# When the spread of a block's maximum is read back from its PSUM bank, in a fused window attention and gated feed-forward kernel

## The chip, the core and the metric

The kernel runs on one core of a Trainium2 chip. TensorE (PE in the profile) multiplies matrices into PSUM, VectorE (DVE) and ScalarE (ACT) work on SBUF and PSUM, GpSimd (POOL) works on SBUF, and SyncE (SP) issues the DMAs. Each engine takes its instructions in the order in which they stand in the program and waits for others by semaphores. The metric is the device time of one execution in microseconds (us).

## The reference

A softmax over 7 window weights for each token and head mixes 7 neighbouring rows of `x`; the result goes through a feed-forward layer with a sigmoid gate. There are 16384 tokens of width 192 and a hidden width of 2048.

```python
def _attn_ref(x, weight_gen):                 # x (4, 4096, 192), weight_gen (4, 4096, 8, 7)
    w = np.exp(weight_gen - np.max(weight_gen, axis=-1, keepdims=True))
    w = w / (np.sum(w, axis=-1, keepdims=True) + 1e-09)
    ...
    out = np.einsum('bshk,bskhg->bshg', w, x_unf)

def _moe_ref(x, w_in, w_out):                 # x (16384, 192)
    h = x @ w_in                              # (16384, 2048)
    g = h * (1.0 / (1.0 + np.exp(-1.702 * h)))
    return (g @ w_out).astype(np.float32)
```

## The kernel before

**Tiling.** The 16384 tokens are 32 blocks of 512. The hidden width is 16 pieces of 128. A unit is one block with one such piece, so there are 512 units, numbered in order. A unit's hidden values are one PSUM bank (128x512 fp32). Every fp32 operand is held as two fp16 parts, so the products are made of several fp16 matmuls.

**A unit's way.** `whole` (lines 391 to 394) is four 512-column matmuls into the unit's bank. `halves` (lines 403 and 404) adds, for two units at a time, two 64-row matmuls, which run side by side in the two halves of the array; a group has three such pairs. `gate` takes the tanh on ScalarE (line 409) and multiplies on VectorE into the bank (line 410). `split` makes the two fp16 parts, the first on ScalarE (line 415) and the second on VectorE (line 416), and with that the bank is free. `second` (lines 426 to 428) is the second layer: 192-column matmuls into the banks named `o`.

**Groups.** Units go in groups of six after a first group of two, with one hidden bank for each place of a group: unit number modulo 6 picks the bank `h0` to `h5`, and the first unit of a group has `h2`. PE takes in each group: `whole` of the first three units with stretches of `second` for the group before in between, the three pairs of `halves`, and then for each further unit a stretch of `second` and its `whole`. `gate` and `split` follow unit by unit.

**A block's scale.** Before its units begin, a block's attention output (GpSimd, lines 149 and 164) gets a power of two as a scale. `scales` takes the largest absolute value per partition on VectorE (line 234), turns it and reduces it again (lines 202 and 207), and a one-column matmul with ones (line 210) spreads it over all partitions, into a whole PSUM bank: `h2`, or an `o` bank for block 1. VectorE reads that bank back (line 216), which frees it, and makes the scale's bits (lines 220 to 222). Then ScalarE and VectorE scale and split the block (`split_x`, lines 275 and 278), and SyncE turns it by DMA into `xt` and copies part of it into `xd` (`turn`, lines 284 and 288).

**What sets the order.** The order is written by hand: `plan(slots, generator)` lists a time for each step of a generator, counted in units, and `until(t)` in the main loop issues all steps that are due before `t`. `first(n)` is the first unit of the group in which unit `n` lies. For a block whose first group starts at `n`, the matmul of line 210 has the time `n - 7.4` and the read of line 216 the time `n - 7.39`: that is the second group before, place 4 (the fifth unit), at 0.6. In the loop the fifth unit's gate is issued, then steps due before 0.5, then the split of the fourth unit, then steps due before the next whole number:

```python
                gate(u)
                until(n + 0.5 + i)
                if last:
                    split(last)
                last = u
                until(min(n + 1 + i, z - 0.4))
```

In the first three groups VectorE and ScalarE also prepare the second layer's weights (`parts_out`, lines 358, 360 and 378).

Of the kernel before, what the change touches and what calls it, by code (L numbers as in the profile page):

```python
# [22 lines left out]
def conv_attention_then_ffn(  # L23
# [10 lines left out]
    B, S, D = x.shape  # L34
    H, K = wg.shape[2], wg.shape[3]
# [9 lines left out]
    NF = DFF // P  # L45
# [178 lines left out]
    def scales(blk):  # L224

        s = scale[blk] = spool.tile([P, 8], F32, tag="s", name="s")
        t = tops[blk % 2]
        if blk == 0:
            for c, n in ((0, P), (1, C1)):
                nc.vector.tensor_reduce(  # L230
                    t[0:n, c : c + 1], turned[c][0:n, :], axis=AX.X, op=ALU.max, apply_absolute_value=True
                )
        else:
            nc.vector.tensor_reduce(
                t[:, 0:1], xa[blk].rearrange("p j d -> p (j d)"), axis=AX.X, op=ALU.max, apply_absolute_value=True
            )
        e = s[:, 0:1].bitcast(I32)
        yield from top_of(t, e, False, ("h3", "o")[blk] if blk < 2 else "h2")
        yield
        power(e, s[:, 2:3], s[:, 3:4], 263)  # L240
# [165 lines left out]
    def gate(u):  # L406

        t = gpool.tile([P, N], F32, tag="th", name="th", bufs=2)
        nc.scalar.activation(t, hp[u], AF.Tanh, scale=scale[u[0]][:, 4:5])  # L409
        nc.vector.scalar_tensor_tensor(hp[u], t, 1.0, hp[u], ALU.add, ALU.mult)  # L410
# [41 lines left out]
    def plan(slots, gen):  # L452
        for n in slots:
            todo.setdefault(math.floor(n), []).append((n, len(todo), gen))

    def once(fn, *args):
        fn(*args)
        yield
# [12 lines left out]
    def hold(t):  # L471

        nc.gpsimd.tensor_copy(held, t)

    with tc.manual_schedule():
        load_w(0)
        load_x(0, 0, J)
        load_tail(0)
        load_in(0)
        load_in(1)  # L480
        load_x(0, J, XB * J)
        load_in(2)
        load_tail(1)
        load_in(3)
        for c in range(4):
            load_out(c)
        load_w(1)
        load_x(1, 0, XB * J)
        constants()


        w_first = ps_h.tile([P, N], F32, tag="h0", name="w")[:, 0 : J * H * K].rearrange("p (n k) -> p n k", k=K)
        plan((-36.1, -35.7, -35.1, -34.6, -33.6), softmax(0, V, w_first))
        plan((-35.3, -34.7, -33.9, -33.2, -32.0), softmax(1, G_))
        plan((-36.2,), once(warm, 7, ident, P))
        plan((-32.1, -30.4, -27.7, -25.0), attend_first(w_first))
        plan((-24.9, -24, -23, -22, -21, -0.04, -0.03), attend(1))
        plan((-20.5, -18.3, -17.1, -17.1), scales(0))
        plan((-15.7, -13.6), split_first())
        raw = {"t": raw_t, "i": raw_i, "o": [raw_o[:, c * QC : (c + 1) * QC] for c in range(NO)]}  # L500
        for k, c, at, *slots in (
            ("t", 0, 0, -28.6, -23.2, -21.6),
            ("i", 0, 1, -27.4, -21.8, -19.7),
            ("i", 1, 2, -26.2, -18.4, -16.9),
            ("i", 2, 3, -24.6, -16.3, -14.5),
            ("t", 1, 4, -22.3, -14.9, -13.2),
            ("i", 3, 5, -20.4, -12.1, -10.1),
            ("o", 0, 6, -18.5, -10.7, -8.9),
            ("o", 1, 7, -13.9, -9.4, -7.5),
            ("o", 2, 8, -12.0, -7.2, -5.7),  # L510
            ("o", 3, 9, -10.8, -4.8, -0.6),
            ("o", 4, 10, -8.2, -0.05, 1.4),
            ("o", 5, 11, -6.3, 1.45, 1.9),
        ):
            plan(slots, narrow((k, c), raw[k][c], at))
        plan((-8.0, -7.1, -5.8), bound_in())
        plan((-5.0,), scales_gate(0))
        plan((-4.5, -3.5), parts_tail(0))
        plan((-3.8, -2.8), parts_in(0))
        plan((-0.05,), once(hold, w0l[:, DFF - 8 :]))  # L520
        plan((-2.75,), once(warm, 5, w0h, QC))
        plan((-3.2, -2.1), parts_in(1))
        plan((-2.5, -1.4), parts_tail(1))
        plan((-1.9, -0.7), parts_in(2))
        plan((-1.2, -0.06), parts_in(3))
        plan((1.95, 4.6, 4.65), bound_out())
        for c, slots in enumerate(((4.7, 5.2), (5.3, 5.8), (6.2, 6.7), (7.55, 7.9), (7.95, 8.1), (8.2, 8.6))):
            plan(slots, parts_out(c))
        plan((4.66,), scales_out(0))
        plan((7.7, 9.4, 9.45, 9.46), scales(1))  # L530
        plan((9.47,), scales_gate(1))
        plan((9.48,), scales_out(1))
        plan((9.49, 10.6), split_x(1))
        plan((10.65, 12), turn(1))

        for blk in range(2, NB):
            n = first(blk * NF)
            plan([n - 12.2, n - 7.4, n - 7.39, n - 7.38], scales(blk))
            plan([n - 6.28], scales_gate(blk))
            plan([n - 6.26], scales_out(blk))  # L540
            plan([n - 6.3, n - 6.2], split_x(blk))
            plan([n - 6.15, n - 5], turn(blk))
            if blk == 2:
                plan((-0.04, 0.5, 4.9, 6.4, 7.2, 7.25), softmax(blk, G_))
                plan((8.61,), once(lambda: hold(wos[:, NF * D - 8 :])))
                plan([8.62 + k for k in range(K)], attend(blk))
            elif blk == 3:
                plan((5.9, 7.26, 8.7, 10.7, 13.7, 17.6), softmax(blk, G_))
                plan([18 + 2 * k for k in range(K)], attend(blk))
            else:  # L550
                plan([n - 48.2, n - 48.1, n - 42.1, n - 36.15, n - 30.2, n - 30.1], softmax(blk, G_))
                plan([n - 30 + 2.2 * k for k in range(K)], attend(blk))
            if blk % XB == 0 and blk > XB:
                plan([blk * NF - 56.5], load_pair(blk // XB))

        def seconds(six):


            for z in zip(six[::2], six[1::2]):
                blk, f = z[0]  # L560
                for i in range(2):
                    if f in (0, NF - 2):
                        for j in (2 * i, 2 * i + 1):
                            for u in z:
                                second(u, j)
                        if f:
                            store(blk, i, each=blk == NB - 1)
                    else:
                        for j in range(J):
                            second(z[i], j)  # L570
                    yield

        sixes = [units[:few]] + [units[n : n + Q] for n in range(few, len(units), Q)]
        for k, us in enumerate([None] + sixes, -1):
            n, z = (min(todo), 0) if k < 0 else (units.index(us[0]), units.index(us[-1]) + 1)
            steps = sorted((t for i in range(n, z) for t in todo.get(i, ())), key=lambda t: t[:2])

            def until(end):
                while steps and steps[0][0] < end:
                    next(steps.pop(0)[2], None)  # L580

            if k < 0:
                until(z)
                continue
            due = seconds(sixes[k - 1] if k > 2 else sixes[0] + sixes[1] if k == 2 else ())
            early, late = us[:3], us[3:]
            if len(us) < Q:
                early, late = us, []
            for i, u in enumerate(early):
                bank(u)  # L590
                whole(u, True, False)
                if i == 1 or i == 0 and k > 2:
                    next(due, None)
                    until(n + 0.5 + 0.5 * i)
            for u in late:
                bank(u)
            for u, v in zip(us[::2], us[1::2]):
                halves(u, v, u in early, v in early)
            last = None
            for i, u in enumerate(us):  # L600
                if i > 1:
                    next(due, None)
                if u in late:
                    whole(u, False, True)
                gate(u)
                until(n + 0.5 + i)
                if last:
# [4 lines that stand above are left out]
            until(z)  # L612
            for _ in due:
                pass
        for _ in seconds(sixes[-1]):
            pass
# [29 lines left out]
```

## Time and profile before

| | us |
|---|---|
| median of 3 runs | 1102.25 (1102.07 to 1102.97) |
| the profiled execution, its own time | 1101.69 |
| its span, first to last instruction | 1099.7 |
| PE busy in it | 1050.0 (95%) |
| DVE busy | 886.6 (81%) |
| POOL busy | 721.2 (66%) |
| ACT busy | 703.6 (64%) |

The span is one execution as the profiler saw it; the time of that execution is 2.0 us longer than its span. Busy time is the union of the records of an engine. A PE record is longer than the distance to the next one, because matmuls are pipelined and the ends of their records are modelled: so the start of one matmul against the start of the next tells how fast PE goes, and idle time counted from the end of a record is less than what was lost.

### The profile page before, as it was taken

Reading aid. Unit: us, or ns where it says so; the run is one execution under the profiler, and the core shown is the slowest. Engines: PE = TensorE matmul, PEld = TensorE weight load, DVE = VectorE, ACT = ScalarE, POOL = GpSimd, SP = SyncE. Lnnn points to the kernel's source line nnn. Section 1 sums busy time; section 2 is a strip of 40 time slices with the busy share of each in tenths; the row PEclk is TensorE's granted clock in tenths of the full one; section 3 lists DMA queues with packets and bytes.
Section 4 is the critical chain, followed back from the end, with each engine's and each line's share of the span. In section 5 each row is a group of like instructions: output and inputs, shape, how many; then the busy total and the mean of one; then the engine's idle time right before and its main releaser. Section 6 shows DMA issues by size and latency. Waiting matters only on the chain.

```text
span 1099.7 us, 22223 instructions
## 1 busy us (share of the span) xinstructions
PE 1050.0 (95%) x8821; PEld 732.6 (67%) x8821; DVE 886.6 (81%) x1556; ACT 703.6 (64%) x1251; POOL 721.2 (66%) x484
## 2 busy tenths in 40 slices
PE   4579999999999999999999999999999999999998
PEld 3146766676667676667766667666666766676666
DVE  8887877888797888879787877887887788788765
ACT  5765666666666666666666666656666666567655
POOL 4469758686855868685587768558775856786100
PEclk9689999999999999999999999999999999999999
DMA  9300120312012121301212120131212102101010
GB/s 305 119 17 16 39 83 18 91 32 91 15 32 77 32 91 32 87 18 32 76 33 90 32 80 27 32 77 32 88 35 74 33 17 91 33 21 44 15 30 18
DMA packets 73231, 60.71 MB, mean 55 GB/s; under 512 B 60588, under 2 KB 65964, under 8 KB 71592
## 3 DMA queue, kind: packets, MB, share of 16 engines
q1 hardware_dynamic: 73128, 59.30, 18.7%
q8 instruction: 69, 1.13, 0.4%
q14 instruction: 34, 0.28, 0.1%
HBM read 31.96 MB, written 12.58 MB: 41 GB/s over the span
## 4 chain that ended last, share of the span: by engine, by line
PE 83%; DVE 8%; ACT 6%; issue 2%; DMA 0%; ACTq 0%
PE o L426 14%; PE o L427 14%; PE o L428 14%; PE h L391 9%; PE h L392 9%; PE h L394 9%; PE h L393 9%; PE h L403 5%; DVE h L410 4%; ACT th L409 3%; DVE g L416 3%; ACT osb L435 1%; DVE tap L149 0%; ACT abs L337 0%; ACT g L415 0%
## 5 line engine op out<-in xcount | busy, mean ns | idle before, releaser
L426 PE MATMUL o<-wos,g 128*128 128x192 f16 x2048 | 505.7, 247 | 3.2 <-DVE s L216 3.2
L427 PE MATMUL o<-wol,g 128*128 128x192 f16 x2048 | 504.9, 247 | 0.5 <-DVE wol L360 0.5
L428 PE MATMUL o<-woh,g 128*128 128x192 f16 x2048 | 504.8, 246 | 0.0
L410 DVE SCALAR_TENSOR_TENSOR h<-th,h 128x512 f32<-128x512 f32 x512 | 347.0, 693 | 181.7 <-ACT th L409 174.6
L409 ACT ACTIVATE th<-h,s 128x512 f32<-128x512 f32 x512 | 342.4, 686 | 231.8 <-PE h L404 135.8
L416 DVE SCALAR_TENSOR_TENSOR g<-g,h 128x512 f16<-128x512 f16 x512 | 349.2, 682 | 13.7 <-ACT g L415 2.0
L164 POOL TENSOR_TENSOR acc<-acc,prod 128x768 f32<-128x768 f32 x186 | 346.3, 1862 | 14.6
L415 ACT ACTIVATE g<-h 128x512 f16<-128x512 f32 x512 | 305.0, 596 | 44.1 <-DVE h L410 44.1
L149 POOL TENSOR_TENSOR prod<-xb,wb 128x768 f32<-128x768 f32 x186 | 288.9, 1553 | 11.1
L426 PEld LDWEIGHTS <-g 128*128 128x128 f16 x2048 | 200.4, 98 | 75.7 <-issue 35.9
L427 PEld LDWEIGHTS <-g 128*128 128x128 f16 x2048 | 200.6, 98 | 39.5 <-issue 3.2
L391 PE MATMUL h<-xt,w0l 128*128 128x512 f16 x512 | 195.1, 381 | 10.4 <-DVE s L216 10.4
L428 PEld LDWEIGHTS <-g 128*128 128x128 f16 x2048 | 200.7, 98 | 0.8 <-issue 0.7
L394 PE MATMUL h<-xt,wth 128*128 128x512 f16 x512 | 195.1, 381 | 0.0
L393 PE MATMUL h<-xt,w0h 128*128 128x512 f16 x512 | 195.1, 381 | 0.0
L392 PE MATMUL h<-xt,w0h 128*128 128x512 f16 x512 | 195.1, 381 | 0.0
L143 POOL TENSOR_TENSOR wb<-wb,wr 128x224 f32<-128x224 f32 x31 | 17.9, 576 | 229.1 <-DVE wr L140 225.6
L278 DVE SCALAR_TENSOR_TENSOR xs<-acc,s,xs 128x512 f16<-128x512 f32 (+1 forms) x62 | 102.3, 1689 | 0.0
L394 PEld LDWEIGHTS <-wth 128*128 128x128 f16 x512 | 50.3, 98 | 61.1 <-issue 1.1
L393 PEld LDWEIGHTS <-w0h 128*128 128x128 f16 x512 | 50.2, 98 | 61.1 <-issue 1.1
L403 PE MATMUL h<-xt,tl 64*128 64x512 f16 x256 | 70.6, 381 | 2.4 <-DVE g L416 2.4
L404 PE MATMUL h<-xd,tl 64*128 64x512 f16 x256 | 70.7, 381 | 2.0 <-DVE g L416 2.0
(92 smaller groups left out, 523.2 us busy)
## 6 DMA issues: line engine op xcount, KB each, us to landing
xb<-in_x_dram SPq DMA_DIRECT2D x12, 1344.0 KB, 6.4
out_dram<-osb SPq DMA_DIRECT2D x31, 384.0 KB, 2.4
wb<-in_weight_gen_dram SPq DMA_DIRECT2D x16, 224.0 KB, 3.2
ro<-in_moe_w_out_dram SPq DMA_DIRECT2D x4, 768.0 KB, 12.3
xb<-in_x_dram SPq DMA_DIRECT2D x3, 768.0 KB, 7.4
ri<-in_moe_w_in_dram SPq DMA_DIRECT2D x4, 512.0 KB, 8.6
xb<-in_x_dram SPq DMA_DIRECT2D x4, 504.0 KB, 5.2
xd<-xt SPq DMA_DIRECT2D x31, 64.0 KB, 2.1
```

The costliest lines, as they stand in the source:

```text
L164: nc.gpsimd.tensor_tensor(acc, acc, t, ALU.add)
L391: nc.tensor.matmul(ps, lhsT=w0l[:, s], rhs=x0, start=start, stop=False)
L392: nc.tensor.matmul(ps, lhsT=w0h[:, s], rhs=x2, start=False, stop=False)
L393: nc.tensor.matmul(ps, lhsT=w0h[:, s], rhs=x0, start=False, stop=False)
L394: nc.tensor.matmul(ps, lhsT=th_[:, s], rhs=x1, start=False, stop=stop)
L409: nc.scalar.activation(t, hp[u], AF.Tanh, scale=scale[u[0]][:, 4:5])
L410: nc.vector.scalar_tensor_tensor(hp[u], t, 1.0, hp[u], ALU.add, ALU.mult)
L415: nc.scalar.activation(g[:, 0], hp[u], AF.Copy, scale=2.0**-12)
L416: nc.vector.scalar_tensor_tensor(g[:, 1], g[:, 0], -(2.0**12), hp.pop(u), ALU.mult, ALU.add)
L426: nc.tensor.matmul(o, lhsT=lo, rhs=wos[:, d], start=a and j % 2 == 0, stop=False, skip_group_check=True)
L427: nc.tensor.matmul(o, lhsT=hi, rhs=wol[:, d], start=False, stop=False, skip_group_check=True)
L428: nc.tensor.matmul(o, lhsT=hi, rhs=woh[:, d], start=False, stop=z, skip_group_check=True)
```

## The change

Nothing is computed in another way. The diff gives three kinds of steps other places in the order.

- For blocks 2 to 31 the spread and its read are due at `n - 7.9` and `n - 7.89`, the three bit operations at `n - 7.3`. A new `until(n + 0.25 + i)` ahead of every gate issues steps that are due in the first quarter of a place. With both, matmul and read stand ahead of the fifth unit's gate; the bit operations stay behind the fourth unit's split.
- For block 1 (`scales(1)`) the spread and its read are due at 8.9 and 8.91 in place of 9.4 and 9.45, which is before the third `whole` of that group.
- Some weight preparation of the second group moves: the steps at 8.1 and 8.6 of the last two `parts_out` come at 8.92 and 8.96, the start of block 2's attention comes at 8.97, and the new `until` lets steps due in a first quarter (at 5.2, 6.2 and 7.2) pass one gate.

```diff
-        for c, slots in enumerate(((4.7, 5.2), (5.3, 5.8), (6.2, 6.7), (7.55, 7.9), (7.95, 8.1), (8.2, 8.6))):
+        for c, slots in enumerate(((4.7, 5.2), (5.3, 5.8), (6.2, 6.7), (7.55, 7.9), (7.95, 8.92), (8.2, 8.96))):
             plan(slots, parts_out(c))
         plan((4.66,), scales_out(0))
-        plan((7.7, 9.4, 9.45, 9.46), scales(1))
+        plan((7.7, 8.9, 8.91, 9.46), scales(1))
...
-            plan([n - 12.2, n - 7.4, n - 7.39, n - 7.38], scales(blk))
+            plan([n - 12.2, n - 7.9, n - 7.89, n - 7.3], scales(blk))
...
-                plan((8.61,), once(lambda: hold(wos[:, NF * D - 8 :])))
-                plan([8.62 + k for k in range(K)], attend(blk))
+                plan((8.97,), once(lambda: hold(wos[:, NF * D - 8 :])))
+                plan([8.98 + k for k in range(K)], attend(blk))
...
+                until(n + 0.25 + i)
                 gate(u)
                 until(n + 0.5 + i)
```

VectorE's order before, in the group in which block 2's maximum is read. The names: `h` and `th` are the hidden bank and its tanh (line 410 is a gate), `g` the fp16 parts (line 416 is a split), `top` the bank with the spread maximum and `s` the block's scale. `h_994` is the fifth unit of the group:

```order
L410 SCALAR_TENSOR_TENSOR h_993<-th_1050,h_993 128x512
L416 SCALAR_TENSOR_TENSOR g_1053<-g_1053,h_988 128x512
L410 SCALAR_TENSOR_TENSOR h_994<-th_1072,h_994 128x512
L416 SCALAR_TENSOR_TENSOR g_1078<-g_1078,h_993 128x512
L216 TENSOR_SCALAR s_939<-top_1081 128x1
L220 TENSOR_SCALAR s_939<-s_939 128x1
```

The same place on VectorE now:

```order
L410 SCALAR_TENSOR_TENSOR h_993<-th_1050,h_993 128x512
L416 SCALAR_TENSOR_TENSOR g_1053<-g_1053,h_988 128x512
L216 TENSOR_SCALAR s_939<-top_1075 128x1
L410 SCALAR_TENSOR_TENSOR h_994<-th_1078,h_994 128x512
L416 SCALAR_TENSOR_TENSOR g_1081<-g_1081,h_993 128x512
L220 TENSOR_SCALAR s_939<-s_939 128x1
```

The read has moved ahead of one gate and one split; so it is in all of blocks 2 to 31, and PE's order is the same there.

PE's order before, around block 1's spread. The names: `o` is a bank of the second layer, `top_624` the spread in an `o` bank, `xd` and `xt` the block's input:

```order
L403 MATMUL h_610<-xt_314,tl_114 128x512
L404 LDWEIGHTS tl_114
L404 MATMUL h_611<-xd_317,tl_114 128x512
L210 LDWEIGHTS ones_92
L210 MATMUL top_624<-tf_566,ones_92 128x1
L426 LDWEIGHTS g_443
L426 MATMUL o_640<-wos_99,g_443 128x192
```

The same matmul on PE now:

```order
L428 LDWEIGHTS g_446
L428 MATMUL o_582<-woh_97,g_446 128x192
L210 LDWEIGHTS ones_92
L210 MATMUL top_597<-tf_566,ones_92 128x1
L391 LDWEIGHTS w0l_95
L391 MATMUL h_607<-xt_314,w0l_95 128x512
L392 LDWEIGHTS w0h_94
L392 MATMUL h_607<-xt_314,w0h_94 128x512
```

The spread has moved ahead of the third `whole` of the group and the six matmuls of `halves` behind it; it is the one place where PE's order differs.

## Rows read from the trace of the kernel before

**Rows 1.** The page's first part: busy time of each engine, share of span, instructions.

```profile
PE 1050.0 (95%) x8821; PEld 732.6 (67%) x8821; DVE 886.6 (81%) x1556; ACT 703.6 (64%) x1251; POOL 721.2 (66%) x484
```

**Rows 2.** The waits: engine, line, waited for; total, times, longest (us).

```profile
PE h L391 <- DVE s L216: 10.4, 30, 0.3
PE o L426 <- DVE s L216: 3.2, 1, 3.2
```

**Rows 3.** Timeline around 420 us: start, length (us), engine, line; idle before, releaser.

```profile
418.66 0.17 PE L210 MATMUL top<-tf,ones 128*128 128x1 bf16 x1
...
419.64 0.70 DVE L410 SCALAR_TENSOR_TENSOR h<-th,h 128x512 f32<-128x512 f32 x1 [0.57 <-ACT th L409]
...
420.24 0.68 DVE L416 SCALAR_TENSOR_TENSOR g<-g,h 128x512 f16<-128x512 f16 x1
...
420.32 0.38 PE L394 MATMUL h<-xt,wth 128*128 128x512 f16 x1
...
420.84 0.15 DVE L216 TENSOR_SCALAR s<-top 128x1 int32<-128x1 int32 x1
...
421.05 0.38 PE L391 MATMUL h<-xt,w0l 128*128 128x512 f16 x1 [0.35 <-DVE s L216]
...
421.26 0.38 PE L392 MATMUL h<-xt,w0h 128*128 128x512 f16 x1
```

**Rows 4.** Timeline: PE at the first and the last of the 30 such places.

```profile
103.54 0.38 PE L394 MATMUL h<-xt,wth 128*128 128x512 f16 x1
...
104.26 0.38 PE L391 MATMUL h<-xt,w0l 128*128 128x512 f16 x1 [0.34 <-DVE s L216]
...
1041.39 0.38 PE L394 MATMUL h<-xt,wth 128*128 128x512 f16 x1
...
1042.11 0.38 PE L391 MATMUL h<-xt,w0l 128*128 128x512 f16 x1 [0.35 <-DVE s L216]
```

**Rows 5.** Timeline of DVE before the fifth gate of another such group, around 163 us.

```profile
163.13 0.68 DVE L416 SCALAR_TENSOR_TENSOR g<-g,h 128x512 f16<-128x512 f16 x1
163.82 0.69 DVE L410 SCALAR_TENSOR_TENSOR h<-th,h 128x512 f32<-128x512 f32 x1
```

**Rows 6.** Timeline, two deliveries that PE needs soon: a turned block, a freed bank.

```profile
699.80 0.62 SPq L288 DMA_DIRECT2D xd<-xt  x1
...
700.83 0.38 PE L391 MATMUL h<-xt,w0l 128*128 128x512 f16 x1
...
508.00 1.44 DVE L416 SCALAR_TENSOR_TENSOR g<-g,h 128x512 f16<-128x512 f16 x2
...
511.07 0.38 PE L404 MATMUL h<-xd,tl 64*128 64x512 f16 x1
```

**Rows 7.** Timeline of the start, 57 to 85 us, around block 1's spread.

```profile
57.12 0.24 PE L427 MATMUL o<-wol,g 128*128 128x192 f16 x1 [0.52 <-DVE wol L360]
...
65.45 0.16 PE L210 MATMUL top<-tf,ones 128*128 128x1 bf16 x1 [0.72 <-DVE tf L207]
...
66.66 1.24 ACT L409 ACTIVATE th<-h,s 128x512 f32<-128x512 f32 x2
...
68.77 0.32 PE L426 MATMUL o<-wos,g 128*128 128x192 f16 x1 [3.15 <-DVE s L216]
...
72.23 0.38 PE L391 MATMUL h<-xt,w0l 128*128 128x512 f16 x1
...
80.12 0.62 SPq L288 DMA_DIRECT2D xd<-xt  x1
...
84.66 0.38 PE L403 MATMUL h<-xt,tl 64*128 64x512 f16 x1
```

**Rows 8.** Stretches: window, length, busy time and count by engine, PE's granted clock, DMA.

```profile
61.60:71.90 10.30, 4.75 (x24) 3.30 (x24) 9.16 (x22) 8.72 (x16) 6.40 (x6) 0.50 0.00 0
80.00:1095.00 1015.00, 1004.65 (x8557) 704.15 (x8556) 817.84 (x1414) 647.74 (x1146) 681.41 (x443) 1.00 0.17 48
```

**Rows 9.** The page's sixth part, DMA issues: count, KB each, us to landing.

```profile
xd<-xt SPq DMA_DIRECT2D x31, 64.0 KB, 2.1
```

## The prediction

> **What bounds the kernel now.** I read the page's busy times first, then the list of waits, then the timeline at the longest PE waits, and last the stretches with the granted clock. TensorE bounds it: PE is busy for 95% of the span and no other engine for more than 81% [rows 1]. So what counts is where PE stands still. The list of waits has two entries that concern the read of a block's maximum (line 216): PE's first `whole` matmul of a group waits for it 30 times, 10.4 us in all, and one `second` matmul waits 3.2 us [rows 2]. The 30 are blocks 2 to 31, the one is block 1.
>
> The timeline shows how such a wait comes about [rows 3]. The spread (line 210) is done on PE at 418.66 + 0.17 = 418.83. VectorE then takes the fifth unit's gate at 419.64, the fourth unit's split at 420.24, and only then the read, at 420.84. It needs 0.15 us, and PE's next group starts 0.06 us behind it, at 421.05, because its first unit has the same bank `h2`. PE had issued its last matmul before that at 420.32.
>
> What was lost is not the 0.35 us that the row calls idle. The end of a matmul's record is modelled; the start of the next tells more. At 421.05 and 421.26 two 512-column matmuls start 0.21 to 0.22 us apart [rows 3], so without the wait the group would have started at 420.54, and 0.51 us were lost. The first and the last of the 30 places have 0.72 us between the two starts, so 0.50 to 0.51 lost [rows 4]. PE runs at the full 2.4 GHz there: the granted clock of the stretch from 80 to 1095 us is 1.00 [rows 8].
>
> **The change part by part.** *Blocks 2 to 31.* PE's order is unchanged; VectorE takes the read ahead of one gate and one split. In the group shown [rows 3] VectorE is idle for 0.57 us before the gate, that is from 419.07, and the spread is in its bank at 418.83. So the read runs from about 419.07 to 419.22, in that idle time, and costs nothing. The bank is free some 1.3 us before PE wants it at 420.54, and the wait goes: 30 times 0.505 to 0.51 us, **15.2 us**.
>
> What is queued behind the read on VectorE is the fifth gate. In some groups, as block 4's, VectorE has no idle time: the split starts at 163.13, the gate at 163.82 [rows 5]. There the gate comes later by the read, 0.15 to 0.2 us, and so does the split behind it; the bit operations follow that split without the read in between, so from there on nothing is later. Who waits for these two results is PE, in the next group. The smallest distance I found between a split and the PE matmul that takes its bank is 511.07 - (508.00 + 1.44) = 1.6 us [rows 6], so 0.2 us is covered.
>
> What is late next? PE comes 0.51 us sooner to everything that hangs on a chain of its own, and the closest is the turned block `xt`. The copy to `xd` is issued as soon as `xt` has landed, so block 20's landed just before 699.80, and PE takes it at 700.83 [rows 6]: 1.0 us, of which 0.5 remains. Ten blocks (2, 5, 8 and so on) begin with a group and are close like this; the others begin inside one and have microseconds more.
>
> *A rule against the trace.* The trace has 0.21 to 0.22 us between matmuls [rows 3]. The Trainium skill, "TensorE: Matmul & The Clock Gate", section "Back-to-back issue gap", says that in a stream of weight loads and matmuls 512 columns take about 131 ns each, and 216 ns only when isolated. By its first figure each wait would cost 0.73 - 0.13 = 0.60 us and the sum would be 17.9 in place of 15.2 us; the trace bears out the second one.
>
> *Block 1.* Its spread takes an `o` bank. Before, `second` waits for the read until 68.77 [rows 7]. Now the spread stands on PE ahead of one `whole` and three pairs of `halves`, and the read on VectorE ahead of two weight preparations and two gates. The spread cannot start before VectorE has the maximum, and that chain does not hang on the work behind it: it starts at about 65.45 as before [rows 7]. So the wait is exchanged: PE now stands still until 65.45 and does the seven slots (four `whole`, three pairs) after it. The granted clock from 61.60 to 71.90 is 0.50 (1.2 GHz) after PE had stood still or been sparsely used [rows 8], so a slot takes 2 x 0.216 = 0.43 us, and seven 3.0 us. `second` would start at 65.45 + 3.1 = 68.6, against 68.77: 0.2 us gained.
>
> The rest depends on the clock. Before, PE worked without a break from 68.77 and was at the full clock from 71.90, 3.1 us later [rows 7, 8]. If the clock comes back as long after 65.45, it is back at 68.6, and the 3.1 us of `second` that ran at half the clock shrink by 1.6: gain 1.8 us. If it comes back at 71.90 all the same, the gain is 0.2; if it comes 3.1 us later still, half of that, 1.6, is lost: -1.4. The Trainium skill's page "TensorE: Matmul & The Clock Gate", section "HAM oscillation — how this bites in real kernels", warns of idle gaps between matmuls because the array then starts cold again. This change makes one longer gap of several shorter ones; by that rule the work behind it starts cold, which the sum above has, and warms up with sustained work, which is the upper end.
>
> A second brake: the first gates of that group wait for the `halves`. Their tanh was at 66.66 [rows 7]; now it cannot start before spread, `whole` and one pair, 65.6 + 5 x 0.43 = 67.8, so about 1.2 us later. Behind it come the split of block 1, its turn and the copy to `xd`, issued at 80.12 [rows 7] and landing 2.1 us later [rows 9]: 82.2 becomes 83.4, and PE, which used it at 84.66, would be there at 82.9. That costs 0.5 of the 1.8. I take **1.0 us**, between 0.2 and 1.3, nearer to the upper end because the trace shows a clock that returns after resumed work; the bounds are -1.4 and 1.8.
>
> *The other moved steps* (weight preparation one gate earlier or later, block 2's attention after 8.97) lie on VectorE, ScalarE and GpSimd in the first 70 us. The early one takes away PE's 0.52 us for `wol` at 57.12 [rows 7], but PE then waits for the spread at 65.45 anyway: nothing. SyncE's order is the same.
>
> **Sum.** 15.2 + 1.0 = 16.2 us. The profiled execution took 1101.69 us, 2.0 more than its span; it becomes 1085.5. The median of the runs is 0.56 us above it, so I forecast **1086.0 us**, 1.5% less.
>
> **The rivals.**
> - *The wait moves to the turned block.* If `xt` lands 1 us later than here, ten blocks give back up to 0.51 us each, 5.1 in all: 1091.1. For it: one of the ten has only 1.0 us. Against: most of those microseconds are still there after the change.
> - *The idle figure is the whole loss.* Then the 30 waits are worth 10.4 and the sum is 11.4: 1090.8. Against: the distances of starts [rows 3].
> - *The closer spacing* of 131 ns: 17.9 + 1.0 = 18.9 us, 1083.3. Against: the pairs of starts [rows 3, 4].
> - *The bank comes back no sooner*, because VectorE reaches the read late in spite of its place: only block 1's part remains, about 1101.2. Against: VectorE's 0.57 us of idle time [rows 3] and the gate at 163.82 [rows 5], both well before the bank is wanted.
> - *Slower.* VectorE takes its instructions in order, so a read that waits for PE's spread holds the fifth gate, the splits, and with them the banks. It decides once the read ends more than 1.6 us after the gate could have run; from there each block pays the excess, and 0.61 us of excess (18.4 / 30) makes the kernel slower by 0.2%. With 0.8 us it is 1086.0 + 24 = 1110. Against: spread and gate's tanh both follow the same `whole`, and the spread ends 0.8 us before the gate starts [rows 3].
>
> **How the numbers follow.** About 0.2% (2.2 us) is what a measurement here can tell from no change. Forecast 0.87, turned block 0.04, idle figure 0.03, closer spacing 0.01, no sooner 0.03, slower 0.02. Faster: 0.87 + 0.04 + 0.03 + 0.01 = 0.95; same 0.03; slower 0.02. The range goes from block 1 at its upper bound (1085.2) and the 0.9 us between runs, 1084.0, to block 1 at its lower bound (1088.4) with some 1.6 us lost at turned blocks, 1090.0.
>
> **What would show it.** In the profile after, the 30 waits of `whole` for line 216 are gone and the starts of lines 394 and 391 at these places are 0.216 us apart; the gate waits for its tanh as before. Block 1's spread starts near 65.5 and has `halves` behind it, and the clock's return there says which end of -1.4 to 1.8 holds. I am wrong if PE shows a new wait of about 0.5 us per block, for `xt`, `xd` or a split.

## The result, and the profile after

The changed kernel took **1085.17 us** (median of 4 runs, 1084.96 to 1086.78) against 1102.53 us before on the same chip (median of 4 runs, 1102.07 to 1102.97). The ratio is 0.9846, with a 95% interval of 0.9829 to 0.9863: 17.4 us or 1.5% faster. 1086.0 was forecast, with 1084.0 to 1090.0 as its range.

The profiled execution of the changed kernel took 1086.78 us with a span of 1084.8 us; it is the highest of the four times, and the profiled execution of before (1101.69) lies below all four of its own. So these two traces differ by 14.9 us of span (1099.7 to 1084.8), and not by 17.4. The page's first line after the change:

```profile
PE 1044.9 (96%) x8821; PEld 732.6 (68%) x8821; DVE 877.9 (81%) x1556; ACT 702.0 (65%) x1251; POOL 722.3 (67%) x484
```

PE bounds the kernel as it did [rows 1], with the same number of instructions, in a span that is 15 us shorter. In the list of waits (engine, line, waited for; total, times, longest, in us) both entries of PE for line 216 [rows 2] are gone. What has grown is PE's wait for the last reduction of block 1's maximum (line 207), one of 8.3 us where [rows 7] has 0.72:

```profile
PE top L210 <- DVE tf L207: 10.5, 2, 8.3
```

This is the group of [rows 3] in the timeline after the change (start, length in us; idle time before it and what ended it):

```profile
413.88 0.17 PE L210 MATMUL top<-tf,ones 128*128 128x1 bf16 x1
...
414.21 0.15 DVE L216 TENSOR_SCALAR s<-top 128x1 int32<-128x1 int32 x1
...
414.86 0.70 DVE L410 SCALAR_TENSOR_TENSOR h<-th,h 128x512 f32<-128x512 f32 x1 [0.50 <-ACT th L409]
...
415.47 0.68 DVE L416 SCALAR_TENSOR_TENSOR g<-g,h 128x512 f16<-128x512 f16 x1
...
415.55 0.38 PE L394 MATMUL h<-xt,wth 128*128 128x512 f16 x1
...
415.76 0.38 PE L391 MATMUL h<-xt,w0l 128*128 128x512 f16 x1
...
415.98 0.38 PE L392 MATMUL h<-xt,w0h 128*128 128x512 f16 x1
```

The read starts 0.33 us behind the start of the spread, in VectorE's idle time, and ends at 414.36. The gate still waits for its tanh (0.50 us of idle time are left of 0.57), and PE's next group starts 0.21 us after line 394, in step. The bank was free 1.40 us before that. (In 20 of the 30 groups this margin is 1.35 to 1.40 us; in the ten in which VectorE is closer packed it is 0.84 or 0.85.) The first and the last of the 30 places, beside [rows 4]:

```profile
103.82 0.38 PE L394 MATMUL h<-xt,wth 128*128 128x512 f16 x1
104.04 0.38 PE L391 MATMUL h<-xt,w0l 128*128 128x512 f16 x1
...
1026.99 0.38 PE L394 MATMUL h<-xt,wth 128*128 128x512 f16 x1
1027.21 0.38 PE L391 MATMUL h<-xt,w0l 128*128 128x512 f16 x1
```

0.72 us became 0.22 at both. Where the two traces part is best told at block 1's first `whole`, since the 30 places all lie behind it. In the timeline of before, and then in that of after, this matmul is:

```profile
83.48 0.38 PE L391 MATMUL h<-xt,w0l 128*128 128x512 f16 x1
```

```profile
83.76 0.38 PE L391 MATMUL h<-xt,w0l 128*128 128x512 f16 x1
```

From there to the end before had 1099.7 - 83.48 = 1016.2 us and after has 1084.8 - 83.76 = 1001.0. The difference is 15.2 us = 30 x 0.506: all the gain of this pair of traces, and 0.28 us more than it, because after reached this point 0.28 us later. So block 1's part gave nothing in the profiled execution. Its timeline, beside [rows 7], and its stretches, beside [rows 8] (window, length; busy time and count of PE, PEld, DVE, ACT, POOL; PE's granted clock; DMA share, GB/s):

```profile
65.93 0.16 PE L210 MATMUL top<-tf,ones 128*128 128x1 bf16 x1 [8.30 <-DVE tf L207]
65.96 0.59 PE L391 MATMUL h<-xt,w0l 128*128 128x512 f16 x1
...
68.40 1.26 ACT L409 ACTIVATE th<-h,s 128x512 f32<-128x512 f32 x2 [1.46 <-PE h L404]
...
69.15 0.34 PE L426 MATMUL o<-wos,g 128*128 128x192 f16 x1
...
72.51 0.38 PE L391 MATMUL h<-xt,w0l 128*128 128x512 f16 x1
...
80.67 0.62 SPq L288 DMA_DIRECT2D xd<-xt  x1
```

```profile
61.80:72.00 10.20, 6.07 (x29) 3.43 (x29) 7.97 (x19) 7.66 (x14) 6.03 (x6) 0.50 0.00 0
72.00:1084.00 1012.00, 1009.23 (x8648) 711.96 (x8646) 817.55 (x1424) 651.93 (x1157) 690.53 (x448) 1.00 0.17 48
```

The wait of 3.15 us behind the spread is gone, but the one ahead of it is 8.30 us long, the spread comes 0.48 us later than before, the work behind it runs at half the clock until 72.00, and the next `whole` starts at 72.51 instead of 72.23.

### The profile page after: what moved, and what is told of

The parts are those of the page before. It is cut to its first block, busy times and chain, and to the rows that moved or that the text cites. A ratio compares the mean times of both kernels' runs of the same rounds, so it can differ in the third digit from the quotient of the medians.

```text
span 1084.8 us, 22222 instructions
## 1 busy us (share of the span) xinstructions
PE 1044.9 (96%) x8821; PEld 732.6 (68%) x8821; DVE 877.9 (81%) x1556; ACT 702.0 (65%) x1251; POOL 722.3 (67%) x484
## 4 chain that ended last, share of the span: by engine, by line
PE 94%; DVE 2%; ACT 2%; issue 1%; DMA 0%; ACTq 0%
PE o L426 16%; PE o L427 16%; PE o L428 16%; PE h L394 10%; PE h L392 10%; PE h L393 10%; PE h L391 10%; PE h L403 6%; DVE tap L149 0%; ACT abs L337 0%; ACT bits L326 0%; DVE g L416 0%; DVE h L410 0%; DMA wb<-in_weight_gen_dram 0%; DVE m L332 0%
## 5 line engine op out<-in xcount | busy, mean ns | idle before, releaser
L426 PE MATMUL o<-wos,g 128*128 128x192 f16 x2048 | 505.3, 247 | 0.0
L426 PEld LDWEIGHTS <-g 128*128 128x128 f16 x2048 | 200.5, 98 | 75.9 <-issue 36.1
L143 POOL TENSOR_TENSOR wb<-wb,wr 128x224 f32<-128x224 f32 x31 | 17.9, 576 | 222.6 <-DVE wr L140 219.7
L278 DVE SCALAR_TENSOR_TENSOR xs<-acc,s,xs 128x512 f16<-128x512 f32 (+1 forms) x62 | 96.5, 1595 | 0.0
```

The source lines that it names most:

```text
L426: nc.tensor.matmul(o, lhsT=lo, rhs=wos[:, d], start=a and j % 2 == 0, stop=False, skip_group_check=True)
```

## The experiments

The main theory: in blocks 2 to 31 each wait had cost the distance of starts less one pitch, 0.505 us. Its rivals: the loss is the idle figure (0.345 us), or the gain comes from something else. A second question is what block 1's part is worth and why. In the short diffs, `-` is the kernel before where nothing else is said.

### Blocks 2 to 31 alone

```diff
-            plan([n - 12.2, n - 7.4, n - 7.39, n - 7.38], scales(blk))
+            plan([n - 12.2, n - 7.9, n - 7.89, n - 7.3], scales(blk))
...
+                if k > 2:
+                    until(n + 0.25 + i)
                 gate(u)
```

> Only blocks 2 to 31 are changed (spread and read ahead of the fifth gate); block 1 and all else of the first three groups stand as before. Theory (what is lost at each of the 30 places is the distance of the starts, 0.73 - 0.22 = 0.51 us, and nothing takes its place): 15.2 us less than before, 1087.3 us at a median of 1102.5. Rival (only the idle time that the profile counts is lost, 0.35 us each): 10.4 us less, 1092.1 us. In the profile PE has no wait of line 391 for line 216 but keeps the one wait of 3.2 us of line 426.

Measured: 1086.48 us (1086.18 to 1087.15, 4 runs) against 1102.53 (13 runs); ratio 0.9856 (0.9841 to 0.987), 16.05 us less. From block 1's first `whole` to the end its trace has 1001.1 us, as the changed kernel's (1001.0). The 30 waits are worth what the distances of starts said (15.2 us; the interval is 14.3 to 17.5), and the idle figure falls: 10.4 us is outside the interval. Block 1's wait is still there in the list of waits of this kernel:

```profile
PE o L426 <- DVE s L216: 3.1, 1, 3.1
```

### Block 1 alone

```diff
-        for c, slots in enumerate(((4.7, 5.2), (5.3, 5.8), (6.2, 6.7), (7.55, 7.9), (7.95, 8.1), (8.2, 8.6))):
+        for c, slots in enumerate(((4.7, 5.2), (5.3, 5.8), (6.2, 6.7), (7.55, 7.9), (7.95, 8.92), (8.2, 8.96))):
...
-        plan((7.7, 9.4, 9.45, 9.46), scales(1))
+        plan((7.7, 8.9, 8.91, 9.46), scales(1))
...
-                plan((8.61,), once(lambda: hold(wos[:, NF * D - 8 :])))
-                plan([8.62 + k for k in range(K)], attend(blk))
+                plan((8.97,), once(lambda: hold(wos[:, NF * D - 8 :])))
+                plan([8.98 + k for k in range(K)], attend(blk))
...
+                until(n + 0.25 + i)
                 gate(u)
```

> Only the first three groups are changed (block 1's spread and read, the moved weight preparation, steps passing a gate); blocks 2 to 31 are read as before. Theory (PE exchanges the wait for the read against a longer wait for the maximum, and what it is worth hangs on when the clock comes back): between 0.3 us more, as in the profiled execution of the changed kernel, and 1.8 us less than before; the 30 waits of 0.35 us stay. Rival (the moved read is a plain gain, the 3.2 us of the wait): 3.2 us less.

Measured: 1101.09 us (1099.94 to 1101.95, 10 runs) against 1102.53 (13 runs); ratio 0.9987 (0.9977 to 0.9996), 1.4 us less (0.4 to 2.5). So the rival, a plain gain of 3.2 us, is out. The list of waits keeps the 30 as they were [rows 2], so nothing of block 1's part touches them. The two parts add up: 16.05 + 1.4 = 17.5 us, against 17.4 for the whole change.

### The read behind the fifth gate, ahead of one split

```diff
-            plan([n - 12.2, n - 7.4, n - 7.39, n - 7.38], scales(blk))
+            plan([n - 12.2, n - 7.9, n - 7.89, n - 7.3], scales(blk))
```

Without the new `until` the read passes the fourth unit's split only.

> As e1_blocks_only, but without the new issuing point ahead of the gate: the read then stands behind the fifth gate and ahead of the fourth split, so it passes one instruction in place of two. Theory (the bank is needed only when PE's next group comes): the read starts where the split did, 420.24 in the trace before, and the bank is free at 420.24 + 0.15 + 0.06 = 420.45, 0.09 us before PE wants it at 420.54; same time as e1_blocks_only within 1 us, 15 us less than before. Rival (the place ahead of the gate is what brings the gain): about half of the wait stays, 7 to 8 us less than before.

Measured: 1086.98 us (1086.34 to 1087.57, 4 runs); ratio 0.9859 (0.9845 to 0.9874). That is 0.5 us beside the kernel that also passes the gate (1086.48), and the two overlap. Its timeline in the same group:

```profile
415.59 0.69 DVE L410 SCALAR_TENSOR_TENSOR h<-th,h 128x512 f32<-128x512 f32 x1 [0.57 <-ACT th L409]
416.20 0.15 DVE L216 TENSOR_SCALAR s<-top 128x1 int32<-128x1 int32 x1
416.27 0.68 DVE L416 SCALAR_TENSOR_TENSOR g<-g,h 128x512 f16<-128x512 f16 x1
...
416.27 0.38 PE L394 MATMUL h<-xt,wth 128*128 128x512 f16 x1
416.49 0.38 PE L391 MATMUL h<-xt,w0l 128*128 128x512 f16 x1
```

The read ends at 416.35, 0.14 us before PE starts the next group, and PE needs 0.06 us behind it [rows 3]. In all 30 groups of this trace the margin is 0.14 or 0.15 us. One split passed is enough for the whole gain, and only just; the gate passed as well takes the margin to between 0.83 and 1.40 us and buys no time here. The rival, that half of the wait stays, is out.

### The read one gate later

```diff
-            plan([n - 12.2, n - 7.4, n - 7.39, n - 7.38], scales(blk))
+            plan([n - 12.2, n - 7.4, n - 6.95, n - 6.94], scales(blk))
```

The read and the bit operations now stand behind the sixth unit's gate.

> As before, but in blocks 2 to 31 the read and the bit operations stand one gate later, behind the sixth unit's gate. That gate waits for its tanh until 421.5 in the trace before, so the read comes at 422.11 in place of 420.84 and PE's next group 1.27 us later. Theory (PE is the bound and pays every such delay in full): 30 x 1.27 = 38 us more than before, 1140.6 us, and 53.4 us more than e1_blocks_only (30 x 1.78 between starts). Rival for the size (the counted idle time is the loss): 30 x 1.62 = 48.6 us more than e1_blocks_only. Rival (later work absorbs a part, because the second layer's matmuls could catch up): clearly less than 38 us more than before.

Measured: 1140.33 us (1140.27 to 1140.93, 4 runs); ratio 1.0344 (1.0329 to 1.036): 37.8 us more than before, and 53.85 more than the kernel without the waits (1086.48). The wait in its list, and one of the 30 in its timeline:

```profile
PE h L391 <- DVE s L216: 48.8, 30, 1.6
```

```profile
408.05 0.38 PE L394 MATMUL h<-xt,wth 128*128 128x512 f16 x1
...
409.86 0.15 DVE L216 TENSOR_SCALAR s<-top 128x1 int32<-128x1 int32 x1
...
410.06 0.38 PE L391 MATMUL h<-xt,w0l 128*128 128x512 f16 x1 [1.62 <-DVE s L216]
```

By the starts each wait costs 410.06 - 408.05 - 0.216 = 1.79 us, and 30 of them 53.8: the runs say 53.85. By the idle figure it would be 48.8, 5 us too little. Nothing of it was absorbed by later work. Each idle figure is too small by the same amount here and before (1.79 - 1.63 = 0.16; 0.505 - 0.345 = 0.16), which is the record's length of 0.38 us less the pitch of 0.216. This one position of a 0.15 us read is worth 54 us between its two ends.

### The changed kernel once more

No edit: the kernel of the change, run beside the next ones.

> The changed kernel once more, on the chip on which the next three run: 1085 to 1087 us.

Measured: 1085.47 us (1084.59 to 1086.21, 4 runs) against 1103.05 (7 runs); ratio 0.9843 (0.9828 to 0.9857). Against the kernel with blocks 2 to 31 alone (1086.48), which ran on another chip, block 1's part is worth 1.0 here and 1.3 in the first measurement (1085.17); with each kernel taken against the kernel before on its own chip it is 17.6 - 16.05 = 1.5 here.

### PE kept busy ahead of block 1's spread

In the changed kernel, 36 matmuls of 512 columns stand ahead of the spread and fill most of the 8.30 us in which PE waits. They write the spread's own bank, which the spread then overwrites: their results are used nowhere. (The line numbers behind them are 3 higher: L407 is line 404.)

```diff
+        if free == "o" and not exact:
+            for _ in range(36):
+                nc.tensor.matmul(ps, lhsT=w0h[:, 0:P], rhs=w0h[:, 0:N], start=True, stop=True)
```

> The changed kernel with 36 matmuls of 512 columns put on PE ahead of block 1's spread, into the bank of that spread (their results are overwritten and used nowhere): 7.8 us of work in the 8.3 us in which PE stands still from 57.6 to 65.9 in the profile of the changed kernel. Theory (what block 1's part costs there is the half clock of the work behind the spread): the clock stays at the full level, the seven slots take 1.5 in place of 3.0 us and the 3.3 us of second layer behind them 1.7, so 2.9 us less than the profiled execution of the changed kernel (1086.8), 1083.9 us. Rival (the chain on ScalarE and VectorE bounds that stretch): no change.

Measured: 1084.19 us (1083.71 to 1084.6, 4 runs); ratio 0.9831 (0.9817 to 0.9846), 1.3 us less than the changed kernel beside it (1085.47). The stretch from 44.70 us on now has the full clock, and PE has a new wait, for block 1's input:

```profile
44.70:1082.00 1037.30, 1030.47 (x8764) 721.83 (x8762) 838.37 (x1473) 672.75 (x1195) 701.82 (x457) 1.00 0.17 49
```

```profile
82.88 0.37 PE L407 MATMUL h<-xd,tl 64*128 64x512 f16 x1 [0.47 <-DMA xd<-xt]
```

The fourth `whole` of the group starts at 69.60 instead of 72.51, and block 1's first `whole` at 80.85 instead of 83.76: the low clock did cost the 2.9 us that were expected. But the input comes no sooner (the copy to `xd` is issued at 80.60, in the changed kernel at 80.67), and PE now stands before it. From block 1's first `whole` to the end this trace has 1082.7 - 80.85 = 1001.9 us against 1001.0, so between the two profiled executions 2.1 us are left. By the medians it is 1.3; that fits the profiled execution of the changed kernel, which ran longer at the low clock behind its spread than the second one (6.1 and 5.1 us, see below). The list of waits has one more entry that the changed kernel lacks, 0.9 us for `wos`; it lies at 55.73 us, ahead of the added matmuls, and is not their doing. So the clock set the time up to 72 us, and once it is full, the input is the next limit, 1.3 us below.

### Block 1's read ahead of the gates instead, PE's order as before

```diff
-        for c, slots in enumerate(((4.7, 5.2), (5.3, 5.8), (6.2, 6.7), (7.55, 7.9), (7.95, 8.1), (8.2, 8.6))):
+        for c, slots in enumerate(((4.7, 5.2), (5.3, 5.8), (6.2, 6.7), (7.55, 9.3), (7.95, 9.31), (8.2, 9.32))):
...
-        plan((7.7, 9.4, 9.45, 9.46), scales(1))
+        plan((7.7, 9.0, 9.01, 9.46), scales(1))
...
-            plan([n - 12.2, n - 7.4, n - 7.39, n - 7.38], scales(blk))
+            plan([n - 12.2, n - 7.9, n - 7.89, n - 7.3], scales(blk))
...
-                plan((8.61,), once(lambda: hold(wos[:, NF * D - 8 :])))
-                plan([8.62 + k for k in range(K)], attend(blk))
+                plan((9.33,), once(lambda: hold(wos[:, NF * D - 8 :])))
+                plan([9.34 + k for k in range(K)], attend(blk))
...
+                if k > 2:
+                    until(n + 0.25 + i)
+                elif k == 2 and i == 0:
+                    until(9.1)
                 gate(u)
```

The spread stays behind the `halves`, as before; its read passes the three weight preparations and the two gates that stood ahead of it on VectorE.

> Blocks 2 to 31 as in the change; block 1's spread stays behind the six matmuls of halves on PE as before, and its read goes ahead of three weight preparations and two gates on VectorE, which follow it. Theory (PE loses at block 1 what the read is late): the read comes at 65.7 in place of 68.56 in the trace before and the second layer at 65.9 in place of 68.77: 2.9 us less than e1_blocks_only (1086.5), 1083.6 us. Rival (the preparations then delay block 1's input, and PE waits for it instead): at most 1 us less than e1_blocks_only.

Measured: 1084.15 us (1083.96 to 1084.3, 4 runs); ratio 0.9831 (0.9816 to 0.9846). All four runs are below all four of the changed kernel on the same chip (1084.59 to 1086.21).

> e6_read_first once more, beside e8_read_first_busy: 1084.1 us within 0.5.

Measured again: 1083.86 us (1083.48 to 1084.46, 4 runs) against 1102.54 (9 runs); ratio 0.9832 (0.9819 to 0.9846). It **beats both kernels**, the changed one by 1.3 us (1085.47 and 1084.15, on one chip). The theory gave 2.9 us less than with blocks 2 to 31 alone. Taken against the kernel before on the same chip each time, the two runs give 2.85 and 2.6 us, and the rival's 1 us at most is out. In the timeline of this second run:

```profile
64.49 0.16 PE L210 MATMUL top<-tf,ones 128*128 128x1 bf16 x1 [0.72 <-DVE tf L207]
64.90 0.32 PE L426 MATMUL o<-wos,g 128*128 128x192 f16 x1 [0.25 <-DVE s L216]
```

The wait behind the spread went from 3.15 to 0.25 us, and the one ahead of it stayed at 0.72, as in [rows 7], and did not become the changed kernel's 8.30: PE has its `whole` and `halves` to do while VectorE makes the maximum.

### The same with weight preparation later still

Here `-` is the kernel just described:

```diff
-        for c, slots in enumerate(((4.7, 5.2), (5.3, 5.8), (6.2, 6.7), (7.55, 9.3), (7.95, 9.31), (8.2, 9.32))):
+        for c, slots in enumerate(((4.7, 5.2), (5.3, 5.8), (6.2, 6.7), (7.55, 9.3), (7.95, 10.61), (8.2, 10.62))):
...
-                plan((9.33,), once(lambda: hold(wos[:, NF * D - 8 :])))
+                plan((9.33,), once(lambda: hold(wos[:, 4 * QC - 8 : 4 * QC])))
```

> As e6_read_first, with two of the three weight preparations behind block 1's scaling and split, so that its input comes 1.5 us earlier. If the input is late in e6_read_first: up to 1.5 us less than it. If not: the same time, about 1083.6 us.

Measured: 1086.87 us (1086.77 to 1087.56, 4 runs); ratio 0.9858 (0.9841 to 0.9874). The kernel is 2.7 us slower than with 9.31 and 9.32, where the same time or up to 1.5 us less was expected. PE has a new wait for a split at block 1's first `whole`, and the timelines show what came late:

```profile
PE h L391 <- DVE g L416: 1.7, 1, 1.7
```

```profile
75.22 4.25 DVE L360 SCALAR_TENSOR_TENSOR wol<-ro,sc,woh 128x512 f16<-128x512 f32 x2
```

```profile
79.80 0.23 ACT L138 ACTIVATE wm<-wm 128x32 f32<-128x32 f32 x1 [8.10 <-DVE wm L134]
```

```profile
80.63 0.70 DVE L410 SCALAR_TENSOR_TENSOR h<-th,h 128x512 f32<-128x512 f32 x1 [0.87 <-ACT th L409]
```

The preparation that was moved out of the way of one chain stands ahead of the next one. The two moved steps take 4.25 us on VectorE; ScalarE waits for a result behind them (`wm`) before it makes its next tanh, and the gate comes at 80.63, in the kernel just described at 76.22. So the split that follows frees its bank late. The list also has a wait of 1.4 us for `wos` (line 426 for line 378) that the kernel just described lacks. It is not the move's: it lies at 55.26 us, ahead of the moved steps, and the kernel with blocks 2 to 31 alone has the same 1.4 us at 55.61. It stands in the traces whose clock stayed full from 50 to 55 us.

### The same with PE kept busy

In the kernel with block 1's read ahead of the gates, 18 matmuls of 512 columns, whose results are used nowhere, stand in front of and between the matmuls of that group's last two pairs of `halves`. (L414 is line 404 here, and L426 is line 416.)

```diff
+    def fill(u, n):
...
+        for _ in range(n):
+            nc.tensor.matmul(filled[0], lhsT=w0h[:, 0:P], rhs=w0h[:, 0:N], start=True, stop=True)
...
     def halves(u, v, last_u, last_v):
+        fill(u, 8 if u == (0, 12) else 0)
...
+        fill(u, 8 if u == (0, 10) else 2 if u == (0, 12) else 0)
```

> As e6_read_first, with 18 idle matmuls of 512 columns (0.22 us each, results used nowhere) in the three gaps that PE has between 58.7 and 63.5 us while it waits for splits. Theory (the half clock from 63.5 to 70.3 us costs PE half of the 5 us in which it has work there): up to 2.5 us less than e6_read_first, less what block 1's input is then late; it landed at 81.4 in that trace, and PE would want it at about 80, so about 1.2 us less: 1082.9 us. Rival (the input bounds this stretch already): no change.

Measured: 1083.86 us (1083.67 to 1084.94, 5 runs); ratio 0.9834 (0.982 to 0.9847), the same as without the extra matmuls; the 1.2 us less that were expected did not come, and the rival (the input bounds this stretch already) holds. The stretch from 41.60 us on has the full clock, and block 1's first `whole` starts at 79.02 instead of 80.54, but PE waits there and behind it where it didn't:

```profile
41.60:1081.00 1039.40, 1029.92 (x8753) 720.60 (x8751) 839.79 (x1477) 673.08 (x1197) 704.60 (x459) 1.00 0.18 49
```

```profile
79.02 0.39 PE L391 MATMUL h<-xt,w0l 128*128 128x512 f16 x1 [0.63 <-DMA xt<-xs]
...
81.26 0.37 PE L414 MATMUL h<-xd,tl 64*128 64x512 f16 x1 [0.67 <-DVE wm L128]
...
400.87 0.38 PE L391 MATMUL h<-xt,w0l 128*128 128x512 f16 x1 [0.64 <-DVE g L426]
```

The first wait is for block 1's turned input. The second is put down to line 128, but this matmul takes `xd`, whose copy is issued at 78.99 and lands some 2.1 us later [rows 9]: it is the input again. Without the extra matmuls that copy is issued at 78.92, so the input does not come sooner when PE does. The third is a single wait for a split much later, whose cause stays open. From block 1's first `whole` to the end this trace has 1081.9 - 79.02 = 1002.9 us, the one without the extra matmuls 1081.6 - 80.54 = 1001.1: the lead is given back.

Three ways to shorten the start (PE busy, the read first, both) end at 1083.9 to 1084.2 us. With both, PE waits for block 1's input: what VectorE and ScalarE make and the DMA turns is then the limit, and neither clock nor read.

## Why the prediction was right, step by step

**Blocks 2 to 31: right, in size and in reason.** 15.2 us was the sum of 30 times 0.505 to 0.51; from block 1's first `whole` on the traces differ by 15.2. That the loss goes by the distance of starts and not by the idle figure is shown by two kernels, one that takes the waits away and one that makes them 1.29 us longer each.

**The rule on closer spacing.** In the stream after the change 512-column matmuls start 0.21 and 0.22 us apart (415.55, 415.76, 415.98 above). The Trainium skill, "TensorE: Matmul & The Clock Gate", section "Back-to-back issue gap", has 131 ns for such a stream; by it the 30 places would have given 17.9 us, as an estimate. No trace here shows that spacing, and 15.2 decides for 216 ns.

**What was queued behind the read: said too high.** The gate was to come 0.15 to 0.2 us later in groups where VectorE has no idle time. In such a group of after:

```profile
354.19 0.69 ACT L409 ACTIVATE th<-h,s 128x512 f32<-128x512 f32 x1
...
354.23 0.68 DVE L416 SCALAR_TENSOR_TENSOR g<-g,h 128x512 f16<-128x512 f16 x1
354.82 0.15 DVE L216 TENSOR_SCALAR s<-top 128x1 int32<-128x1 int32 x1
354.92 0.70 DVE L410 SCALAR_TENSOR_TENSOR h<-th,h 128x512 f32<-128x512 f32 x1
```

Split and gate start 0.69 us apart with the read between them, and 0.69 apart without it [rows 5]. But these groups do have a little spare time, which the prediction missed: the gate starts 0.04 us behind the end of its tanh here (354.88), and 0.03 behind it in [rows 5], where the tanh is:

```profile
163.10 0.69 ACT L409 ACTIVATE th<-h,s 128x512 f32<-128x512 f32 x1
```

So the tanh sets the gate in both, and the read fits in ahead of it. Where the read stands between two operations of which the second does not wait, it has a price: with the read behind the gate, gate and split start 0.67 or 0.68 us apart in all 30 groups, and without it 0.60 (419.64 and 420.24 in [rows 3]). That is 0.07 us, not 0.15 to 0.2. The cover of 1.6 us was not needed.

**What is late next: right.** No new wait of PE in the steady part. Block 20's turned block, the closest, had 1.0 us [rows 6] and was to keep 0.5. After the change (the copy to `xd` is issued as `xt` lands):

```profile
691.09 0.61 SPq L288 DMA_DIRECT2D xd<-xt  x1
...
691.50 0.38 PE L391 MATMUL h<-xt,w0l 128*128 128x512 f16 x1
```

0.4 us are left. By that, another 0.5 us out of PE's time at this place would meet this chain.

**Block 1: the size held, three of its terms did not.** 1.0 us was taken; the runs give 1.0 to 1.5, and the pair of profiled executions 0.28 us the other way. The terms were the start of the spread, the return of the clock and the late input, and that their errors leave 1.0 is luck in part. The table has the times (in us) that the following rests on, in the seven traces with either order:

| trace | spread before it on PE | block 1's spread | low clock (0.50) | block 1's first `whole` |
|---|---|---|---|---|
| before | 50.32 | 65.45 | 61.60 to 71.90 | 83.48 |
| blocks 2 to 31 alone | 49.68 | 64.81 | 62.20 to 72.40 | 83.41 |
| read behind the gate | 50.12 | 65.27 | 63.90 to 74.10 | 84.49 |
| read one gate later | 49.93 | 65.07 | 63.40 to 73.70 | 84.17 |
| changed | 50.45 | 65.93 | 61.80 to 72.00 | 83.76 |
| changed, once more | 49.70 | 65.20 | 60.10 to 70.30 | 82.56 |
| block 1 alone | 50.12 | 65.61 | 60.60 to 70.80 | 83.02 |

The first four have block 1's order as before, the last three the new one.

*The spread* did not start "as before": it came at 65.93 and not 65.45. The spread before it on PE (of the scale of the second layer's weights) lies ahead of all moved steps; in the timelines of before and after:

```profile
50.32 0.16 PE L210 MATMUL top<-tf,ones 128*128 128x4 bf16 x1 [0.41 <-DVE tf L205]
```

```profile
50.45 0.16 PE L210 MATMUL top<-tf,ones 128*128 128x4 bf16 x1 [0.41 <-DVE tf L205]
```

From there to block 1's spread it takes 15.13 to 15.15 us in all four traces of the order before, and 15.48 to 15.50 in all three of the new one. So 0.35 of the 0.48 us belong to the new order, and 0.13 were there at 50 us. What differs between is weight preparation that now passes gates on VectorE and ScalarE, which make the maximum's input; I had called those steps free because PE waits for the spread anyway, and it is this spread that they delay. Which of them does it was not tried by itself.

*The clock's return* was sized by one execution: 3.1 us after resumed work [rows 7, 8]. In the trace of after it is 72.00 - 65.93 = 6.1 us. The stretches of low clock in the changed kernel's second run and in the kernel with block 1 alone:

```profile
60.10:70.30 10.20, 5.10 (x23) 2.51 (x23) 8.59 (x20) 7.65 (x15) 5.06 (x6) 0.50 0.00 0
```

```profile
60.60:70.80 10.20, 5.18 (x24) 2.53 (x24) 8.68 (x20) 7.66 (x15) 5.15 (x6) 0.50 0.00 0
```

There the clock is back 5.1 and 5.2 us after the spread. And in three more kernels with block 1 as before (blocks 2 to 31 alone; the read behind the gate; the read one gate later):

```profile
62.20:72.40 10.20, 5.66 (x29) 4.10 (x30) 9.06 (x21) 7.47 (x14) 7.47 (x7) 0.50 0.00 0
```

```profile
63.90:74.10 10.20, 6.29 (x31) 4.40 (x32) 9.06 (x19) 6.23 (x11) 7.58 (x7) 0.50 0.00 0
```

```profile
63.40:73.70 10.30, 6.19 (x31) 4.39 (x31) 9.16 (x19) 6.53 (x12) 7.68 (x7) 0.50 0.00 0
```

In these it is back 7.6, 8.8 and 8.6 us after their spreads; in the trace of before it was 6.5, the earliest of the four. All seven stretches are 10.2 or 10.3 us long. What differs is where they begin: 1.4 to 3.9 us ahead of the spread in the order before, and 4.1 to 5.1 us ahead of it in the new one, where PE stood still for the 8.3 us before the spread. So in these seven the clock is back sooner after the spread because it fell sooner, and the time since work resumed, by which the prediction went, does not tell. Why the stretch lasts as long as it does is left open: in both runs with the read first, in which PE does not wait 3.15 us behind its spread, it is 6.7 us (63.10 to 69.80 in the second).

*The input* was to cost 0.5 us, since the first tanh behind the spread would come 1.2 us later and the copy to `xd` with it. The tanh came 1.7 us later (68.40 and 66.66), the copy only 0.55 (80.67 and 80.12), and PE's list has no wait for it: those 0.5 us were not paid.

From the spread before to block 1's first `whole` the table has 33.2 to 34.4 us in the order before, 33.9 on average, and 32.9 to 33.3 in the new one, 33.0 on average. So 0.9 us of gain by seven traces, beside 1.0 to 1.5 by the medians, and none in the pair of traces that the page shows: that of before has the shortest way of its four and that of after the longest of its three.

**The rivals.** The turned block (1091.1), the idle figure (1090.8) and a bank that is no sooner free (1101.2) fall with the 15.2 us. So does the slower case: the gate starts 0.98 us behind the start of the spread (414.86 and 413.88), as in [rows 3], so the read held nothing. What lies between forecast and median (1086.0 and 1085.17) is less than the scatter of the four runs.

## What to carry to other kernels

A short read that frees a PSUM bank belongs in its engine's order as early as its input is there, not where its result is used: 0.15 us of read cost 0.5 us of TensorE a time when it stood behind one split, 1.8 us behind one gate more, and nothing a split earlier. Price such a wait by the starts of the matmuls around it less their usual pitch; the idle figure of the row is too small by the record's length less the pitch. What one execution shows of the start of a kernel, where the clock changes, needs a second trace before a term of a sum rests on it. And look up when a wait in a list took place before you put it down to an edit: the 1.4 us for `wos` came ahead of the moved steps.

## What the hardware showed that was not expected

- The clock's return differs from execution to execution at the same order. Behind the gap PE ran again at 1.2 GHz for 3.1 us (before), 4.3, 5.5 and 5.3 us (three kernels with block 1's order as before, counted from `second` at the spread + 3.3 us) and 6.1, 5.1 and 5.2 us (the new order, counted from the spread) until the granted clock went from 0.50 to 1.00. The whole low stretch, with the gap in it, was 10.2 or 10.3 us long in each of these seven.
- A 0.15 us VectorE read between two 512-column operations moves the second by 0.07 us: 0.67 us between their starts with it (30 places), 0.60 without. Where the second waits for its tanh anyway, it moves it by nothing: 0.69 us with and without.
